# A transformer block on one core: score due times kept until issue, x loaded in eight parts

## The chip, the core and the metric

The kernel runs on one core of one Trainium2 chip. The time is the device time of one execution in microseconds (us); the median of three runs is compared. The engines are TensorE (PE), VectorE (DVE), ScalarE (ACT), GpSimd (POOL) and SyncE (SP, which issues the DMAs).

## The reference

One block of a transformer in bf16: attention with 32 heads on 2,048 tokens of width 640 (20 per head), then a gated MLP with hidden width 1,728. B_x is not read.

```python
x = A_x
h = x + _A_ref(_layernorm(x), A_wqkv, A_wo)
    # q, k, v = split(x @ wqkv); p = softmax(q k^T * 20**-0.5); o = p v; o @ wo
h2 = h + _B_ref(_layernorm(h), B_w_gate, B_w_up, B_w_down)
    # (gelu(x @ w_gate) * (x @ w_up)) @ w_down
```

## The kernel before

The program is written by a planner in the kernel file. Every operation is given to `op` with an engine, a planned duration, a priority (a low number goes first), what it reads and writes, and the PSUM banks that it takes and gives back. `Sched.schedule` plays the engines forward in planned time and lays down one order for each engine; `emit` then writes each engine's instructions in that order, with semaphore waits where an operand comes from another engine. So the order on each engine is fixed when the program is built. On the chip an engine that is late delays what stands behind it.

**Front.** x is loaded by `load_x` in four DMAs of four token tiles (128 tokens each), in the order XORD, followed by the weights. Tiles are normalized (statistics of tiles 0 to 10 on DVE, of 11 to 15 on ACT, by `act_stats`), transposed on PE and copied out by ACT or DVE (XN_DVE). K of the first head group is projected for all tokens, a bound for the exponent is worked out from it (`sel0`, `q_bound0`, key ("qo", 0, 0)), and then the first scores can be made. While x comes in, PE runs WN matmuls on zeros (line 607) wherever it has nothing else. HOLD, Q1_HOLD, V_HOLD and K1_AFTER say which of the next K, Q and V projections or copies wait for the bound or for an earlier copy.

**Attention.** Tokens (as queries) are cut into eight chunks (SIZES), and each chunk with a group of heads into slots, 32 in all; several tables (QK_LEAD, PE_AGE, SD_AGE, SD_ROW, D_SLOT, SUMS, D_RING, D_SPAN) have one entry for each slot. A score tile is 128 keys by 512 queries and fills one PSUM bank. Scores are made by PE in "row" mode (line 1059), units alternating between banks 0 to 2 and banks 3 and 4; one ACT instruction takes the exp of a whole unit, 1,536 or 1,024 columns, straight from PSUM, and gives its banks back. So score n+2 can be made when exp n has ended, and has to be there when exp n+1 ends. Of the tiles, 348 go to DVE, which builds the exponential from integer tricks (line 972 and four terms after it; SUMS says how many pairs of terms DVE adds up, which saves PE a PV pass). Such a tile has its scores in one of the banks 5 and 7 or, as D_RING says, in the third bank of a three-bank unit, whose exp is then a short one. PV (line 437 on PE, into bank 6) runs in "col" mode.

**The due time.** PE is also filled with background: projections for later chunks, output projection and MLP of the chunk before (`post`, lines 740, 1314, 1383). To keep it from being in the way of scores, the planner holds a time `due`, and skips a PE operation that would run across it:

```python
if e == "pe" and due is not None and o.prio[0] > 0 and t < due < t + o.dur + (MODE_SWITCH[e] ...):
    skipped.append((p, i))
...
if e == "act":
    act_end = max(act_end, t) + o.dur + ACT_GAP
    due = act_end + (0.917 if o.dur > 1.2 else 1.344) - at(QK_LEAD) if o.mode == "exp" else None
```

It is set anew each time that an operation is issued to ACT. When PE has nothing that it may start, it may run filler matmuls on zeros (`warm`, `pad`), which keep its recent activity above a share.

**After each chunk.** `post` makes the output projection, the layer norm (P_ADD and P_ST are the priorities of its DVE steps), the transposes (on PE for the chunks in XP_PE, by a DMA for the others) and the MLP. The last chunk's `post` runs behind the last exp.

Of the kernel before, what the change touches and what calls it, by code (L numbers as in the profile page):

```python
# [18 lines left out]
DRAIN = {"pe": 0.165, "act": 0.118, "dve": 0.085, "pool": 0.05, "sp": 0.0}  # L19
WARM_WIN, WARM_MIN = 3.4, 0.5  # L20
PAD_WIN, PAD_MIN = 3.4, 0.42
QK_LEAD = (0.68, 0.72, 0.65, 0.6, 0.65, 0.65,) + (0.72,) * 8 + (0.65,) * 3 + (0.72,) * 6 + (0.68,) * 9
ACT_GAP = .012
PE_AGE = (2.5, 3.0, 5.0, 5.0, 2.5,) + (1.0,) * 4 + (2.0,) + (5.0,) * 3 + (3.0,) * 8 + (1.5,) * 6 + (3.5, 3.0,) + (1.5,) * 3
SD_AGE = (0.6, 0.6, 0.3,) + (0.6,) * 6 + (0.8,) + (0.6,) * 3 + (0.5, 0.6, 1.0, 0.3, 0.6, 0.8, 0.6, 1.0, 0.5, 1.0, 1.0, 0.5,) + (0.6,) * 7
SD_ROW = (0,) * 5 + (1.0,) + (0.6,) * 3 + (1.5, 0.6, 0.6, 1.5,) + (0.6,) * 16 + (1.0, 0.6, 0,)
STOP = None


# [1 line left out]
MODE_SWITCH = {"pe": .098, "act": 1.28}  # L31
# [20 lines left out]
class Sched:  # L52
# [47 lines left out]
    def schedule(self):  # L100
# [11 lines left out]
        mode = {e: None for e in ENGINES}  # L112
# [13 lines left out]
        at = lambda v: v[cur] if isinstance(v, tuple) else v  # L126
        total = len(ops)
        scores = sum(o.eng == "pe" and o.mode == "row" for o in ops)
        while done < total:
            assert events, "no operation can start"  # L130
            t = heapq.heappop(events)
# [4 lines left out]
            for e in ENGINES:  # L136
# [8 lines left out]
                while ready[e]:  # L145
                    p, i = heapq.heappop(ready[e])
                    o = ops[i]
                    got = []
                    if e == "pe" and due is not None and o.prio[0] > 0 and t < due < t + o.dur + (MODE_SWITCH[e] if mode[e] not in (None, o.mode) else 0):
                        skipped.append((p, i))  # L150
                        if due not in events:
                            heapq.heappush(events, due)
                        if len(skipped) >= 60:
                            break
                        continue
                    for bk in o.acq:
                        for b in bk.allowed if scores else bk.allowed + bk.after:
                            if owner[b] is None and free_at[b] <= t + 1e-9 and b not in got and b not in kept:
                                got.append(b)
                                break  # L160
                        else:
                            got = None
                            break
                    if got and o.mode == "row" and 0 < p[0] < 1 and scores > 1 and t - o.ready < (
                            at(SD_AGE) if mode[e] != "row" else at(SD_ROW) if row_end[o.rows[0]] > max([row_start + 0.01] + [freed[b] for b in got]) + 0.02 else 0):
                        skipped.append((p, i))
                        continue
                    if got is None:

                        if p[0] == 0:  # L170
                            kept.update(bk.allowed[0] for bk in o.acq)
                        skipped.append((p, i))
                        continue
                    skipped.append((p, i))
                    if chosen is None:
                        chosen, banks = o, got
                        if e != "pe" or p[0] < 1 or p[0] == P_NOW or o.mode == mode[e] or t - o.ready > at(PE_AGE):
# [16 lines left out]
                if chosen is None:  # L194
                    if e == "pe" and self.warm is not None:
                        while recent and recent[0][0] < t - WARM_WIN:
                            recent.popleft()
                        fb = [b for b in self.warm_banks if owner[b] is None and free_at[b] <= t + 1e-9]
                        free7 = fb and all(hasattr(ops[d], "fin") and ops[d].fin + 0.06 <= t for d in self.warm_deps)
                        if sum(x for _, x in recent) < WARM_MIN * WARM_WIN and (free7 or live):  # L200
# [12 lines left out]
                            chosen = o  # L213
                            total += 1
                    if chosen is None:
                        continue
                o = chosen
                scores -= o.eng == "pe" and o.mode == "row"
                if o.tag and o.tag[0] == "S":
                    cur = self.slot_of[o.tag[1]]  # L220
                if e == "pe" and self.pad is not None and o.tag and o.tag[0] in ("O", "Oq"):
# [29 lines left out]
                if e == "act":  # L251
                    act_end = max(act_end, t) + o.dur + ACT_GAP
                    o.fin = act_end + o.lat
                    due = act_end + (0.917 if o.dur > 1.2 else 1.344) - at(QK_LEAD) if o.mode == "exp" else None
                heapq.heappush(events, free[e])
                for bk in o.rel:
                    b = bk.b
# [78 lines left out]
S = 2048  # L336
# [22 lines left out]
NTERM = len(TERMS)  # L359
PV_QUADS = 2  # L360
PR, PR2 = 13, 6
D_SLOT = (1,) + (3,) * 26 + (2, 3, 3, 0, 0,)
SUMS = (0,) + (1,) * 5 + (2, 0, 0, 1, 0,) + (1,) * 3 + (0, 1, 1, 2, 3, 1, 0, 1, 1, 0, 2, 2, 1, 0, 1, 0, 3, 0,)
HOP = 3.2
D_LAT = 0.3
RECIP_MAGIC = float(0x7EF311C3)
COL = 256
WN, WB, WW, WC = 76, (5, 4), 256, 32
VN = 4
D_RING = (9,) * 8 + (6,) * 20 + (12,) + (3,) * 3  # L370
D_FIRST = 0
D_SPAN = (16,) + (18,) * 13 + (17,) + (18,) * 4 + (19,) * 4 + (18,) * 7 + (17, 17,)
D0 = 8
P33 = ()
TANH_FROM = 768
GELU_A = 2.0 * 0.7978845608028654
# [6 lines left out]
P_V0 = 2.91  # L383
P_ON = 2.4
V_ACT = (0, 3)
XN_DVE = (8, 10, 13, 15)
VP = (0, 2, 5, 8)
V1 = ((0, 0, 0, 0, 0, 0, 0, 0, 1, 1, 1, 1, 1, 1, 1, 1), (2, 2, 2, 2, 3, 3, 3, 3, 3, 3, 3, 3, 4, 4, 4, 4))
# [27 lines left out]
def bass_sequential_preLN__mha_block__glu_gated_geglu__prompt_kernel(  # L416
# [12 lines left out]
    with ExitStack() as es:  # L429
# [13 lines left out]
        def c_act(n):  # L443
            return 0.052 + n * 0.000833
# [258 lines left out]


        def act_stats(t0, n):
            for t in sorted(range(t0, t0 + n), key=lambda t: (XORD.index(t // 4), t)):
                for f, k in ((ACT.Copy, 0), (ACT.Square, 1)):
                    op("act", I("activation", junk, x_sb[:, t, :], f, accum_out=asum[:, k, t - t0:t - t0 + 1]), 0.86, 1.4,
                       reads=[f"x{t // 4}"], writes=["junk", ("as", t)])
# [8 lines left out]
        for t0, n in GROUPS:  # L718
            if (t0, n) == AG:
                act_stats(t0, n)  # L720
            else:
                for t in range(t0, t0 + n):
                    ln_stats(x_sb[:, t, :], t, [f"x{t // 4}"], P_BG)
            ln_rsqrt(t0, n, P_RS, sqrt=True)
            for t in range(t0, t0 + n):
                e_ops.append(ln_apply("dve", x_sb[:, t, :], xn_p[:, t % 4, :], ("xnp", t % 4), t, [f"x{t // 4}"], P_PRO))
# [696 lines left out]
        for s_, (c, gs) in enumerate(slots):  # L1423
# [37 lines left out]
            if gs[-1] == NG - 1:  # L1461
# [39 lines left out]
```

## Time and profile before

| | us |
|---|---|
| median of 3 runs (lowest, highest) | 867.11 (866.93, 867.78) |
| profiled execution, its time | 867.46 |
| profiled execution, span of its instructions | 865.7 |
| PE busy | 835.9 |
| ACT busy | 839.4 |
| DVE busy | 748.5 |
| first exp starts | 33.00 |
| table load behind the last exp starts | 842.41 |

The granted TensorE clock reads 1.00 throughout. The groups name an instruction by its line, but line 437 is a helper that issues most instructions of ACT, DVE and SP, so the names of the tiles say more: `pts` and `rege` out of `ps` on ACT are exps, `rege` or `qt_all` out of `ps` on line 972 are tiles of DVE, `ps` out of `pts`, `rege` or `qt_all` with `v_all` on PE is PV, and `ps` out of `kt_all,zer` is filler.

### The profile page before, as it was taken

How to read it: one execution, taken by the hardware profiler on the slowest of the kernel's cores; microseconds unless marked ns; L12 is line 12 of the kernel's file. 1: busy time of each engine (PE TensorE's matmuls, PEld its weight loads, DVE VectorE, ACT ScalarE, POOL GpSimd, SP SyncE). 2: the span in 40 equal slices, each digit the busy share in tenths (PEclk: the TensorE clock that was granted, in tenths of full speed). 3: DMA queues.
4: the chain of work that ended last, by engine and by line, in shares of the span. 5: the costliest groups of instructions: out<-in, count | busy, mean ns of one | idle time of the engine just before them, and what ended most of it. 6: DMA issues, size and time to landing. Idle time of an engine off the chain costs nothing.

```text
span 865.7 us, 35516 instructions
## 1 busy us (share of the span) xinstructions
PE 835.9 (97%) x16187; PEld 420.8 (49%) x16219; DVE 748.5 (86%) x1371; ACT 839.4 (97%) x806; POOL 93.7 (11%) x268
## 2 busy tenths in 40 slices
PE   7999999999999899999999999999999999999998
PEld 5533332322344344445455555555554556666667
DVE  8859999999898899797899989999999897998344
ACT  7899999999999999999999999999999999999992
POOL 5001111110001210101002010011102110010000
DMA  7211122123102442001110201010101201020000
GB/s 274 84 50 57 32 71 61 46 71 93 53 4 67 128 146 80 16 18 36 53 42 16 36 8 61 5 35 17 49 19 24 58 8 31 19 48 11 2 18 17
DMA packets 47485, 42.54 MB, mean 49 GB/s; under 512 B 18628, under 2 KB 41952, under 8 KB 47336
## 3 DMA queue, kind: packets, MB, share of 16 engines
q1 hardware_dynamic: 47336, 40.27, 16.0%
q8 instruction: 127, 2.08, 1.0%
q14 instruction: 22, 0.18, 0.1%
HBM read 27.95 MB, written 10.26 MB: 44 GB/s over the span
## 4 chain that ended last, share of the span: by engine, by line
ACT 45%; PE 42%; DVE 11%; issue 1%; DVEq 0%
ACT pts L437 30%; ACT rege L437 14%; PE ps L1059 13%; PE ps L437 11%; PE ps L740 10%; PE ps L745 3%; DVE qt_all L437 2%; PE ps L887 2%; DVE rege L437 2%; DVE rege L972 2%; PE ps L1314 1%; DVE qt_all L972 1%; DVE stats L437 1%; ACT qt_all L437 1%; PE ps L1383 1%
## 5 line engine op out<-in xcount | busy, mean ns | idle before, releaser
L437 ACT ACTIVATE pts<-ps 128x1024 bf16<-128x1024 f32 (+1 forms) x496 | 558.3, 1232 | 2.9 <-PE ps L1059 2.1
L1059 PE MATMUL ps<-qt_all,kt_all 32*128 32x256 bf16 (+2 forms) x4096 | 307.1, 273 | 11.2 <-ACT pts L437 5.2
L437 ACT ACTIVATE rege<-ps 128x1024 bf16<-128x1024 f32 (+1 forms) x222 | 247.6, 1192 | 0.4 <-PE ps L1059 0.2
L1059 PEld LDWEIGHTS ps<-qt_all,kt_all 32*128 32x128 bf16 x4096 | 104.2, 92 | 198.1 <-ACT pts L437 83.0
L972 DVE TENSOR_SCALAR rege<-ps 128x512 int16<-128x512 f32 x220 | 148.2, 683 | 19.4 <-PE ps L1059 18.1
L437 PE MATMUL ps<-rege,v_all 128*21 128x256 bf16 (+2 forms) x2201 | 140.3, 286 | 1.3 <-DVE rege L437 0.5
L437 PE MATMUL ps<-pts,v_all 128*21 128x256 bf16 (+2 forms) x2403 | 124.7, 273 | 1.0 <-DVE osb L437 0.8
L740 PE MATMUL ps<-rege,regw 128*32 128x256 bf16 (+1 forms) x2600 | 120.5, 296 | 1.5 <-DVE rege L972 0.5
L972 DVE TENSOR_SCALAR qt_all<-ps 128x512 int16<-128x512 f32 x128 | 86.5, 682 | 11.9 <-PE ps L1059 11.4
L437 DVE TENSOR_SCALAR rege<-rege 128x2048 int16<-128x2048 int16 x141 | 94.5, 686 | 2.5 <-PE ps L437 1.9
L740 PEld LDWEIGHTS ps<-rege,regw 128*32 128x32 bf16 x2600 | 60.4, 96 | 34.6 <-issue 20.1
L437 PEld LDWEIGHTS ps<-rege,v_all 128*21 128x21 bf16 x2201 | 54.1, 91 | 42.7 <-issue 25.2
L437 PEld LDWEIGHTS ps<-pts,v_all 128*21 128x21 bf16 x2403 | 57.0, 91 | 26.1 <-issue 18.4
L740 PE MATMUL ps<-regw,rege 128*32 128x320 bf16 x1296 | 68.1, 301 | 0.7 <-issue 0.4
L437 DVE TENSOR_SCALAR qt_all<-qt_all 128x2048 int16<-128x2048 int16 (+4 forms) x113 | 65.4, 589 | 2.8 <-ACT qt_all L437 1.1
L437 PE MATMUL ps<-qt_all,v_all 128*21 128x256 bf16 (+1 forms) x1264 | 56.4, 264 | 0.8 <-DVE qt_all L437 0.8
L437 DVE TENSOR_SCALAR qt_all<-rege 128x2048 int16<-128x2048 int16 x80 | 53.8, 684 | 1.5 <-PE ps L437 0.9
L745 PE MATMUL ps<-regw 128*128 128x512 bf16 x176 | 52.5, 383 | 2.0 <-issue 1.1
L437 POOL TENSOR_SCALAR rn<-rc 128x16 int32<-128x16 int32 x22 | 6.7, 305 | 393.3 <-DMA rc<-sums 393.1
L1368 DVE TENSOR_TENSOR rege<-rege,ps 128x512 bf16<-128x512 bf16 (+2 forms) x53 | 35.0, 661 | 13.0 <-PE ps L740 6.6
L1314 PE MATMUL ps<-rege,regw 128*128 128x128 bf16 (+1 forms) x420 | 41.0, 238 | 0.0
L740 PEld LDWEIGHTS ps<-regw,rege 128*32 128x32 bf16 x1296 | 30.3, 96 | 19.3 <-issue 11.8
(139 smaller groups left out, 806.2 us busy)
## 6 DMA issues: line engine op xcount, KB each, us to landing
bsum<-rsums SPq DMA_DIRECT2D x88, 64.0 KB, 2.0
rege<-in_A_x_dram SPq DMA_DIRECT2D x5, 640.0 KB, 5.9
q_rows<-regw SPq DMA_DIRECT2D x20, 128.0 KB, 1.7
out_dram<-rege SPq DMA_DIRECT2D x15, 160.0 KB, 1.8
regw<-in_B_w_gate_dram SPq DMA_DIRECT2D x5, 432.0 KB, 3.3
regw<-in_B_w_up_dram SPq DMA_DIRECT2D x5, 432.0 KB, 3.4
kt_all<-k_rows SPq DMA_DIRECT2D x12, 160.0 KB
qt_all<-q_rows SPq DMA_DIRECT2D x12, 160.0 KB
```

Source lines behind the costliest of these rows:

```text
L437: return lambda eng: getattr(eng, method)(*args, **kwargs)
L740: return [lambda eng, j=j: eng.matmul(out()[32 * j:32 * j + 32], l[:, 32 * j:32 * j + 32], r, start=start, stop=stop, tile_position=(0, 32 ...
L745: fn = col4(lambda: bank(bk, n), l, r, k == 0, k == len(steps) - 1) if col else lambda eng, l=l, r=r, k=k: eng.matmul(bank(bk, n), l, r, s ...
L887: w_readers.append(op("pe", lambda eng, i=i, kt=kt, a=a: eng.matmul(bank(bk)[:, i * w:i * w + w], xnT[:, a, kt * 128:(kt + 1) * 128], wv[: ...
L972: d_ops.append(op("dve", lambda eng: eng.tensor_scalar(v[:, 512 * h:512 * h + 512], bank(b), EXP_MUL, -32000.0, ALU.mult, ALU.max), c_dve( ...
L1059: return lambda eng: eng.matmul(out()[:, kk * nq:(kk + 1) * nq], kt_all[32 * j:32 * j + 32, g, kt * 128:(kt + 1) * 128], qt_all[32 * j:32 ...
L1314: lambda eng, a=a, f=f, fi=fi: eng.matmul(bank(bk)[:, fi * nq:(fi + 1) * nq], w[:, a, F0[f]:F0[f] + 128], hnT[:, a, 128 * tb:128 * tb + nq ...
L1368: hdone.append(op("dve", lambda eng, bu=bu, fv=fv, w=w: eng.tensor_tensor(fv, fv, bank(bu, w), ALU.mult), c_dve(w), p, reads=[ku] + hkeys( ...
L1383: f == NF - 1) if cl else lambda eng, f=f, o=o, bk=bk, w0=w0, w1=w1: eng.matmul(
```

## The change

- **Due time.** A table `needed` holds the due time of each score by its number, and a score that is issued takes the next one out, so that it stands until that score is issued. The length of the running exp comes from the list of units (`sc.pace`). For GRACE = 0.05 us from the due time on, PE starts no other operation either. QK_LEAD goes from 0.60 to 0.72 down to 0.50 to 0.60. WARM_DUE, which would hold filler matmuls off the due time, is 0.
- **x** is loaded in eight DMAs of two tiles, in the order XORD = (0, 6, 1, 7, 2, 3, 5, 4).
- **WN**, the zero matmuls in front, goes from 76 to 60.
- **Tables.** One tile group for DVE moves from slot 18 to slot 23 (D_SLOT), SUMS rises by one in slots 0, 8 and 17 and falls by one in 19, D_RING rises from 6 to 9 in slots 8, 9, 12 and 13, D0 goes from 8 to 0, and a few entries of PE_AGE, SD_AGE, SD_ROW and D_SPAN change.
- **Order of the front and of `post`.** HOLD 1 to 3 (the second K's copies wait for the bound's end), Q1_HOLD 1 to 0, K1_AFTER 2 to 0, V_HOLD 6 to 4, XN_DVE and V1 changed, P_ADD 0.6 to 1.8, P_ST 1.9 to 0.7, and chunk 6 leaves XP_PE, so that its transpose is a DMA.

```diff
-QK_LEAD = (0.68, 0.72, 0.65, 0.6, 0.65, 0.65,) + (0.72,) * 8 + (0.65,) * 3 + (0.72,) * 6 + (0.68,) * 9
+QK_LEAD = (0.55,) * 9 + (0.5,) + (0.55,) * 9 + (0.5,) + (0.55,) * 10 + (0.6, 0.6,)
+GRACE = 0.05
+WARM_DUE = 0
...
-                    if e == "pe" and due is not None and o.prio[0] > 0 and t < due < t + o.dur + (MODE_SWITCH[e] if mode[e] not in (None, o.mode) else 0):
+                    if e == "pe" and due is not None and o.prio[0] > 0 and (
+                            t < due < t + o.dur + (MODE_SWITCH[e] if mode[e] not in (None, o.mode) else 0) or
+                            GRACE and due <= t < due + at(GRACE)):
...
+                n_exp += o.mode == "exp"
+                if o.tag and o.tag[0] == "S":
+                    n_qk += 1
+                    if GRACE:
+                        due = needed.pop(n_qk, None)
...
-                    due = act_end + (0.917 if o.dur > 1.2 else 1.344) - at(QK_LEAD) if o.mode == "exp" else None
+                    d = act_end + ((0.917 if o.dur > 1.2 else 1.344) if not GRACE or n_exp >= len(self.pace) else self.pace[n_exp]) - at(QK_LEAD) if o.mode == "exp" else None
+                    if GRACE and d is not None and n_qk <= n_exp:
+                        needed[n_exp + 1] = d
+                    elif not GRACE or d is not None:
+                        due = d
...
+        sc.pace = [c_act(512 * len(x)) + ACT_GAP + 0.005 for x in units]
...
-D_SLOT = (1,) + (3,) * 26 + (2, 3, 3, 0, 0,)
-SUMS = (0,) + (1,) * 5 + (2, 0, 0, 1, 0,) + (1,) * 3 + (0, 1, 1, 2, 3, 1, 0, 1, 1, 0, 2, 2, 1, 0, 1, 0, 3, 0,)
+D_SLOT = (1,) + (3,) * 17 + (2,) + (3,) * 4 + (4,) + (3,) * 3 + (2, 3, 3, 0, 0,)
+SUMS = (1,) * 6 + (2, 0, 1, 1, 0,) + (1,) * 3 + (0, 1, 1, 3, 3, 0, 0, 1, 1, 0, 2, 2, 1, 0, 1, 0, 3, 0,)
-WN, WB, WW, WC = 76, (5, 4), 256, 32
+WN, WB, WW, WC = 60, (5, 4), 256, 32
-D_RING = (9,) * 8 + (6,) * 20 + (12,) + (3,) * 3
+D_RING = (9,) * 10 + (6, 6, 9, 9,) + (6,) * 14 + (12,) + (3,) * 3
-D0 = 8
+D0 = 0
-XP_PE = (0, 6)
-HOLD = 1
+XP_PE = (0,)
+HOLD = 3
-K1_AFTER = 2
-Q1_HOLD = 1
-V_HOLD = 6
+K1_AFTER = 0
+Q1_HOLD = 0
+V_HOLD = 4
-XORD = (0, 3, 1, 2)
+XORD = (0, 6, 1, 7, 2, 3, 5, 4)
-P_ADD = 0.6
-P_ST = 1.9
+P_ADD = 1.8
+P_ST = 0.7
...
-            load(x_sb[:, 4 * i:4 * i + 4, :], x_hbm[512 * i:512 * (i + 1), :].rearrange("(t p) d -> p t d", p=128),
-                 f"x{i}", 5.1 + 1.8 * k)
+            load(x_sb[:, 2 * i:2 * i + 2, :], x_hbm[256 * i:256 * (i + 1), :].rearrange("(t p) d -> p t d", p=128),
+                 f"x{i}", 4.2 + 0.9 * k)
```

More of the change, by code (lines that the diff above doesn't have):

```diff
@@ L21 @@
 PAD_WIN, PAD_MIN = 3.4, 0.42
-QK_LEAD = (0.68, 0.72, 0.65, 0.6, 0.65, 0.65,) + (0.72,) * 8 + (0.65,) * 3 + (0.72,) * 6 + (0.68,) * 9
+QK_LEAD = (0.55,) * 9 + (0.5,) + (0.55,) * 9 + (0.5,) + (0.55,) * 10 + (0.6, 0.6,)
+GRACE = 0.05
+WARM_DUE = 0
 ACT_GAP = .012
-PE_AGE = (2.5, 3.0, 5.0, 5.0, 2.5,) + (1.0,) * 4 + (2.0,) + (5.0,) * 3 + (3.0,) * 8 + (1.5,) * 6 + (3.5, 3.0,) + (1.5,) * 3
-SD_AGE = (0.6, 0.6, 0.3,) + (0.6,) * 6 + (0.8,) + (0.6,) * 3 + (0.5, 0.6, 1.0, 0.3, 0.6, 0.8, 0.6, 1.0, 0.5, 1.0, 1.0, 0.5,) + (0.6,) * 7
-SD_ROW = (0,) * 5 + (1.0,) + (0.6,) * 3 + (1.5, 0.6, 0.6, 1.5,) + (0.6,) * 16 + (1.0, 0.6, 0,)
+PE_AGE = (2.5, 3.0, 5.0, 5.0, 2.5,) + (1.0,) * 4 + (2.0, 5.0, 5.0,) + (3.0,) * 9 + (1.5,) * 6 + (3.5, 3.0,) + (1.5,) * 3
+SD_AGE = (0.6, 0.6, 0.3,) + (0.6,) * 6 + (0.8,) + (0.6,) * 3 + (0.5, 0.6, 1.0, 0.3, 0.6, 0.8, 0.6, 1.0, 0.5, 1.0, 1.0, 0.5,) + (0.6,) * 5 + (0.3, 0.6,)
+SD_ROW = (0,) * 5 + (1.0,) + (0.6,) * 3 + (1.5, 0.6, 0.6, 1.5,) + (0.6,) * 11 + (1.0,) + (0.6,) * 4 + (1.0, 0.6, 0,)
 STOP = None
@@ L128, in schedule @@
         scores = sum(o.eng == "pe" and o.mode == "row" for o in ops)
+        n_qk = n_exp = 0
+        needed = {}
         while done < total:
@@ L148, in schedule @@
                     got = []
-                    if e == "pe" and due is not None and o.prio[0] > 0 and t < due < t + o.dur + (MODE_SWITCH[e] if mode[e] not in (None, o.mode) else 0):
+                    if e == "pe" and due is not None and o.prio[0] > 0 and (
+                            t < due < t + o.dur + (MODE_SWITCH[e] if mode[e] not in (None, o.mode) else 0) or
+                            GRACE and due <= t < due + at(GRACE)):
                         skipped.append((p, i))
-                        if due not in events:
+                        if t < due and due not in events:
                             heapq.heappush(events, due)
+                        if t >= due and due + at(GRACE) not in events:
+                            heapq.heappush(events, due + at(GRACE))
                         if len(skipped) >= 60:
@@ L199, in schedule @@
                         free7 = fb and all(hasattr(ops[d], "fin") and ops[d].fin + 0.06 <= t for d in self.warm_deps)
-                        if sum(x for _, x in recent) < WARM_MIN * WARM_WIN and (free7 or live):
+                        x = t + 0.215 + (MODE_SWITCH[e] if not (live and (mode[e] == "col" or not free7)) else 0)
+                        if WARM_DUE and due is not None and t < due < x:
+                            if due not in events:
+                                heapq.heappush(events, due)
+                        elif sum(x for _, x in recent) < WARM_MIN * WARM_WIN and (free7 or live):
                             o = Op()
@@ L367 @@
 COL = 256
-WN, WB, WW, WC = 76, (5, 4), 256, 32
+WN, WB, WW, WC = 60, (5, 4), 256, 32
 VN = 4
-D_RING = (9,) * 8 + (6,) * 20 + (12,) + (3,) * 3
+D_RING = (9,) * 10 + (6, 6, 9, 9,) + (6,) * 14 + (12,) + (3,) * 3
 D_FIRST = 0
-D_SPAN = (16,) + (18,) * 13 + (17,) + (18,) * 4 + (19,) * 4 + (18,) * 7 + (17, 17,)
-D0 = 8
+D_SPAN = (16,) + (18,) * 12 + (17,) * 4 + (18, 18,) + (19,) * 4 + (18,) * 7 + (17, 17,)
+D0 = 0
 P33 = ()
@@ L385 @@
 V_ACT = (0, 3)
-XN_DVE = (8, 10, 13, 15)
+XN_DVE = (9, 11, 13, 15)
 VP = (0, 2, 5, 8)
-V1 = ((0, 0, 0, 0, 0, 0, 0, 0, 1, 1, 1, 1, 1, 1, 1, 1), (2, 2, 2, 2, 3, 3, 3, 3, 3, 3, 3, 3, 4, 4, 4, 4))
+V1 = ((0, 0, 0, 0, 0, 0, 0, 0, 0, 0, 0, 0, 0, 0, 0, 0), (2, 2, 2, 2, 2, 2, 2, 2, 3, 3, 3, 3, 3, 3, 3, 3))
 X_LAT = 3.0
@@ L705, in act_stats @@
         def act_stats(t0, n):
-            for t in sorted(range(t0, t0 + n), key=lambda t: (XORD.index(t // 4), t)):
+            for t in sorted(range(t0, t0 + n), key=lambda t: (XORD.index(t // 2), t)):
                 for f, k in ((ACT.Copy, 0), (ACT.Square, 1)):
                     op("act", I("activation", junk, x_sb[:, t, :], f, accum_out=asum[:, k, t - t0:t - t0 + 1]), 0.86, 1.4,
-                       reads=[f"x{t // 4}"], writes=["junk", ("as", t)])
+                       reads=[f"x{t // 2}"], writes=["junk", ("as", t)])
             m = mv[:, t0:t0 + n, 0]
@@ L722, in bass_sequential_preLN__mha_block__glu_gated_geglu__prompt_kernel @@
                 for t in range(t0, t0 + n):
-                    ln_stats(x_sb[:, t, :], t, [f"x{t // 4}"], P_BG)
+                    ln_stats(x_sb[:, t, :], t, [f"x{t // 2}"], P_BG)
             ln_rsqrt(t0, n, P_RS, sqrt=True)
             for t in range(t0, t0 + n):
-                e_ops.append(ln_apply("dve", x_sb[:, t, :], xn_p[:, t % 4, :], ("xnp", t % 4), t, [f"x{t // 4}"], P_PRO))
+                e_ops.append(ln_apply("dve", x_sb[:, t, :], xn_p[:, t % 4, :], ("xnp", t % 4), t, [f"x{t // 2}"], P_PRO))
                 if t in XD:
```

## The prediction

> **What bounds the kernel now.** I read the page first, then the waits of ScalarE (ACT), the groups by shape, the chain, the timeline around single stalls, and the stages at both ends.
>
> ```profile
> span 865.7 us, 35516 instructions
> PE 835.9 (97%) x16187; PEld 420.8 (49%) x16219; DVE 748.5 (86%) x1371; ACT 839.4 (97%) x806; POOL 93.7 (11%) x268
> ...
> ACT pts L437 <- PE ps L1059: 2.1, 6, 0.6
> ...
> 33.00 3.71 ACT L437 ACTIVATE pts<-ps 128x1536 bf16<-128x1536 f32 x3 [0.64 <-PE ps L1059]
> 842.41 1.28 ACT L437 ACT_TABLE_LOAD   x1
> ```
>
> ACT and TensorE (PE) both read 97%, so the page alone doesn't say which one sets the end. The two last rows cut the run in three: 33.0 us ahead of the first exp, 809.4 us of attention (33.00 to 842.41), and a tail of 865.7 - 842.4 = 23.3 us. The waits of ACT name only 2.1 us of waiting for scores (line 1059). But ACT overlaps the end of one instruction with the start of the next, so a short delay shows as a longer pitch and not as idle time. The pitch stands in the chain, the number of exps in the groups by shape:
>
> ```profile
> 270.80 5.97 ACT pts L437 x5
> 276.77 2.75 ACT rege L437 x3
> 279.52 5.44 ACT pts L437 x5
> ...
> 287.21 5.01 ACT pts L437 x5
> ...
> L437 ACT ACTIVATE pts<-ps 128x1024 bf16<-128x1024 f32 x300 | 306.9, 1065 | 1.2 <-PE ps L1059 0.9
> L437 ACT ACTIVATE pts<-ps 128x1536 bf16<-128x1536 f32 x196 | 291.4, 1487 | 1.8 <-PE ps L1059 1.2
> L437 ACT ACTIVATE rege<-ps 128x1024 bf16<-128x1024 f32 x154 | 156.2, 1061 | 0.1
> L437 ACT ACTIVATE rege<-ps 128x1536 bf16<-128x1536 f32 x68 | 101.1, 1487 | 0.3 <-PE ps L1059 0.2
> L437 ACT ACTIVATE qt_all<-qt_all 128x1024 f16<-128x1024 f16 x13 | 14.2, 1101 | 0.0
> L437 ACT ACTIVATE rege<-rege 128x2048 bf16<-128x2048 bf16 x4 | 7.4, 1903 | 0.0
> L437 ACT ACT_TABLE_LOAD x8 | 10.3, 1283 | 0.9 <-PEq L1486 0.8
> ```
>
> Runs of five differ by their mix: 5.01 is four short exps (1,024 columns) and one long (1,536), 5.44 is three and two. The difference makes long minus short 0.43 us, so the short pitch is 0.916 us (three give the row's 2.75) and the long 1.346. Three long and two short would be 5.87; the row with 5.97 holds 0.10 of waiting that no idle column shows. All exps at these pitches take 454 x 0.916 + 264 x 1.346 = 771.2 us. Other ACT work between the two marks is 14.2 + 7.4 + half of the table loads (5.1) and a few small groups that I put at 5 us together; less an overlap of 0.15 us (1.065 - 0.916) for some 21 of them, about 29 us. 809.4 - 771.2 - 29 leaves about 9 us of score stalls in pieces of 0.05 to 0.6 us. That pool is what the new due time can reach. One such piece:
>
> ```profile
> 86.96 1.99 ACT L437 ACTIVATE rege<-ps 128x1024 bf16<-128x1024 f32 x2
> 88.96 1.45 ACT L437 ACTIVATE pts<-ps 128x1536 bf16<-128x1536 f32 x1
> ...
> 87.76 0.61 PE L437 MATMUL ps<-rege,v_all 128*21 128x512 bf16 x8
> 88.20 0.39 PE L437 MATMUL ps<-pts,v_all 128*21 128x512 bf16 x4
> 88.52 0.60 PE L1059 MATMUL ps<-qt_all,kt_all 32*128 32x512 bf16 x4
> ```
>
> Two short exps start at 86.96 and should end 2 x 0.916 later, at 88.79; the next exp starts at 88.96, 0.17 late. The banks for it came free near 87.88, when the first of the two ended. PE then finished eight PV matmuls, ran four more at 88.20, and only then the scores at 88.52, 0.64 after the release. From scores to exp is 0.44 (88.52 to 88.96), so with a short exp running the scores must start within 0.916 - 0.44 = 0.47 us of the release.
>
> **The change, part by part.** *The due time.* Before, each exp that the planner issues overwrites it, so it is lost just when the banks come free; a tanh wipes it. And it guesses the running exp's length from the last one's: after a short exp it says 1.344 less QK_LEAD (0.60 to 0.72), about 0.65 after the release, which is where this row sits (0.64). The 95 units of which VectorE (DVE) takes one bank are short exps where the guess says long, so some 190 guesses of 718 are wrong. After, the length comes from the unit list, the due time stays until that score is issued, and it is 0.905 + 0.017 - 0.55 = 0.37 us after the release for a short exp. The four matmuls at 88.20 (0.32 after it, until 0.64) would be refused; the scores would start at 88.20, and the 0.17 us go. But 0.37 against 0.47 leaves only 0.10 us for PE to run behind plan, less than where the old rule aimed after a long exp (0.917 less 0.65 to 0.72, 0.2 to 0.27 after the release). So I take 5 of the 9 us: bounds 0 (all is lateness of PE against the plan) and 9.
>
> What waits instead is PE's background, and DVE behind it. It is covered while PE has slack:
>
> ```profile
> 500.00:600.00 100.00, 98.37 (x2474) 1.00 0.10 27
> 600.00:700.00 100.00, 99.05 (x2355) 1.00 0.13 33
> ...
> sum 809.00, PE 787.11; mean PE 87.46
> ...
> 500.00:600.00 100.00, 0.60 (x8) 1.00 0.10 27
> 600.00:700.00 100.00, 0.40 (x4) 1.00 0.13 33
> ...
> sum 809.00, PE 22.73; mean PE 2.53
> ```
>
> The upper rows are PE's stages, the lower ones those of the filler matmuls on zeros. Idle 809.0 - 787.1 = 21.9 and filler 22.7 make 44.6 us, 0.062 us per score of 719; but from 500 to 700 only 1.63 + 0.95 + 1.00 = 3.6 us. What is put off there moves to later stages.
>
> *Tables.* Counted from the tables, 2,048 tiles still split into 1,700 for ACT and 348 for DVE; ACT gets 719 exps for 718 (455 of two banks, 263 of three, one of a single bank): a bank costs 0.43, so the fixed part of an exp is 0.916 - 2 x 0.43 = 0.06 us, and one exp more adds that. Pair sums rise from 27 to 29:
>
> ```profile
> L437 DVE TENSOR_TENSOR qt_all<-qt_all 128x2048 bf16<-128x2048 bf16 x9 | 10.9, 1213 | 0.0
> ```
>
> DVE gains 2 x 1.21 = 2.4 us, PE loses two groups of four PV matmuls (0.22 each, half of 87.76 to 88.20). At 86% busy DVE hides it; uncovered it would cost 2.4. WARM_DUE is 0, so that branch does nothing. The other age and span tables only reorder: 0, bounds -1 and +1.
>
> *The front.*
>
> ```profile
> 0.78 3.03 SPq L437 DMA_DIRECT2D rege<-in_A_x_dram  x4
> 6.55 0.48 DVE L437 MEMSET v_all<- 128x512 bf16 x1 [1.84 <-issue]
> 6.65 1.22 DVE L437 BATCH_NORM_STATS2 stats<-rege 128x6 f32<-128x320 bf16 x3
> 7.23 0.74 ACT L437 ACTIVATE rege<-rege 128x640 bf16<-128x640 bf16 x1 [1.36 <-DMA rege<-in_A_x_dram]
> ...
> 2.92 7.97 PE L607 MATMUL ps<-zer,ident 128*128 128x256 bf16 x47 [2.92 <-POOL ident L437]
> 12.95 0.45 PE L662 MATMUL ps<-ident,rege 128*128 128x128 bf16 x5 [2.06 <-DVE rege L437]
> 14.91 3.05 PE L607 MATMUL ps<-zer,ident 128*128 128x256 bf16 x26
> ...
> 9.00:10.00 1.00, 1.00 (x12) 0.88 (x10) 1.00 (x4) 0.78 (x2) 0.81 (x4) 1.00 1.06 408
> ```
>
> The four parts of x move at 408 GB/s (9 to 10 us), so a part of 320 KB takes 0.8 us where one of 640 took 1.6. ACT waits 1.36 us for its first tile, now in the second half-size part: that goes. DVE carries the chain up to about 20 us; it stood 1.84 us ahead of a memset that waits for no data, so an earlier x may or may not bring it forward. Bounds 0 and -1.84; I take -0.9. SP issues four more DMAs, 0.76 us each by the first row (3.03 for 4), and the weights queue 3 us further back; the same bytes lie ahead of them, so they land as before. The new holds (K and V copies after the first bound) move DVE work behind the first exp: within the same bounds. Of the 16 dropped zero matmuls I expect the last to go, those of the run of 26 at 14.91, where PE waits anyway: 0.
>
> A rule speaks against the eight parts. The Trainium skill ("DMA: Bandwidth & Descriptors", section Bandwidth) says to batch DMAs to 1 MiB for 75% of peak, and its table lies at 138 GB/s for 64 KB and 341 for 1 MB. By an estimate from it, 220 GB/s at 320 KB, the 2.6 MB of x would land 5 us later, and the gain of the front would be 0. The trace disagrees for queued parts: 408 GB/s at 640 KB.
>
> *The tail.*
>
> ```profile
> 803.05 0.45 DVE L437 TENSOR_SCALAR xn_t<-rege,mu,rs 128x640 bf16<-128x640 bf16 x1
> ...
> 814.88 0.49 DVE L1388 TENSOR_TENSOR rege<-ps,rege 128x320 bf16<-128x320 f32 x1 [0.38 <-PE ps L1383]
> rege<-xn_t SPq DMA_TRANSPOSE x10, 3.0
> ...
> 851.52 7.98 PE L1314 MATMUL ps<-rege,regw 128*128 128x128 bf16 x140
> ```
>
> Chunk 6 is transposed by a DMA (3.0 us to land, so near 806.5) in place of PE and a DVE copy, no quicker than 1 us after 803.5. PE is still at chunk 5's down projection at 814.88, which hides the 2 us between; uncovered they are +2. The last chunk's MLP (851.52 on) is unchanged. Tail 0, bounds -0.6 and +2 for background left over.
>
> Sum: -5.0 - 0.9 + 0.06 + 0 = -5.8. The profiled execution took 867.46 us for its span of 865.7, so 861.6; the median of the runs lies 0.35 lower: **861.3**.
>
> **Rivals.** *Given back (0.17).* The stalls go, but the 3.6 us of slack between 500 and 700 are used up and the background is worked off after the last exp. For it: PE at 99% there. Against: 44.6 us free in all. A fifth of the run's stalls would be made up there and at most the 3.6 us missing slack comes back, I say 3: 864.5. *Slower (0.15).* PE held free costs more than it saves. A loss of r per score uses 719 r out of 44.6 us of slack, or 39.6 once the stalls are gone; it decides from 0.055 us. At 0.068 it leaves 9.3 us of background behind the last exp, where PE is already full, less 5.8: 870.6. Against: the due time (0.37) lies behind the release, so a 0.22 us operation mostly fits. *No effect (0.14).* The stalls come from PE running late against its plan, not from the plan. For it: the matmuls at 88.20 start 0.32 after the release, when no plan with the scores ready would pick them. Only the front gains: 866.3. *Cold PE (0.05).* The 47 zero matmuls from 2.92 run at 5.9 per us on the whole and at 12 between 9 and 10 (granted clock 1.00), so PE was at half rate for about 5 us. If fewer of them let it fall back, half of that, 2.5 us, is lost ahead of the first exp: 863.8. The Trainium skill ("TensorE: Matmul & The Clock Gate", part 1) states such a rule: half clock after an idle window of about 3.4 us. By the trace, PE was not slow after its 2.06 us gap (26 zero matmuls in 3.05 us at 14.91), which is why the chance is small.
>
> **How the numbers follow.** The forecast has 0.49, its own range 857 to 865 (9 or 1 us of stalls, front 0 to -1.8). 0.2% is 1.7 us, about what a measurement of this kernel can tell from no change. Faster: 0.49, of "given back" 0.13, of "no effect" 0.04, cold 0.05: 0.71. Same: 0.12 from those two. Slower: 0.15 and 0.02: 0.17. The range 857.0 to 867.5 leaves out the slower case and a little below.
>
> **What would show it.** Right: fewer and smaller steps like 5.97 against 5.87 in ACT's chain, attention of about 804.5 us, first exp near 32.1, tail within 1 us of 23.3. PE rows with PV at 0.3 us behind a release and scores at 0.64 should be gone. Wrong: attention unchanged (PE's lateness), a tail of 26 us or more (given back), filler or idle PE up by over 30 us (reserved stretch too dear), zero matmuls well under 8 per us after 13 us (cold).

## Result and the profile after

The changed kernel took **870.49 us** (median of seven runs, 870.27 to 870.70) against 867.11 (866.66 to 867.78): 1.0034 of the time before, 95% interval 1.0025 to 1.0044. It is slower by 3.4 us; 861.3 was forecast. The profiled execution has the median's time.

The page of the changed kernel, its span and its engines:

```profile
span 868.8 us, 35317 instructions
PE 829.0 (95%) x16080; PEld 417.3 (48%) x16115; DVE 749.4 (86%) x1372; ACT 837.9 (96%) x807; POOL 90.9 (10%) x268
```

ACT in its timeline, at the first exp and at the table load behind the last one, the marks that the prediction used:

```profile
30.68 1.28 ACT L458 ACT_TABLE_LOAD   x1
37.13 4.20 ACT L458 ACTIVATE pts<-ps 128x1024 bf16<-128x1024 f32 x4 [5.17 <-PE ps L1080]
...
844.77 1.28 ACT L458 ACT_TABLE_LOAD   x1
```

ACT's waits (in total, times, longest):

```profile
ACT pts L458 <- PE ps L1080: 6.2, 4, 5.2
```

| us | before | after | difference | forecast |
|---|---|---|---|---|
| ahead of the first exp | 33.00 | 37.13 | +4.13 | -0.9 |
| attention, first exp to table load | 809.41 | 807.64 | -1.77 | -4.9 |
| tail | 23.33 | 23.99 | +0.66 | 0 |
| span | 865.74 | 868.76 | +3.02 | -5.8 |

So attention did get shorter, and the loss is one wait of 5.17 us at the first exp.

For the small waits I took the starts and ends of all exps from both traces. Where nothing holds an exp up, it starts 0.904 us behind the start of a short one (1,024 columns) and 1.330 behind that of a long one (1,536). The ends follow at another pitch: 0.917 us for a short exp and 1.344 for a long one, within 0.005 us of it in 406 of the 441 short and 206 of the 258 long exps after that directly follow another exp. So the starts run ahead of the ends, and a late start need not delay an end. Of the changed kernel, ACT's timeline:

```profile
193.10 2.45 ACT L458 ACTIVATE rege<-ps 128x1024 bf16<-128x1024 f32 x2
195.33 5.22 ACT L458 ACTIVATE pts<-ps 128x1024 bf16<-128x1024 f32 x5
200.42 2.40 ACT L458 ACTIVATE rege<-ps 128x1536 bf16<-128x1536 f32 x2
```

The middle row is four short exps and a long one. At the pitch of starts the next one would follow 4.95 us later; it starts 5.09 later, so it is 0.14 late. But the first row ends at 195.55 and the middle one at 200.55, 5.00 apart, where 4 x 0.917 + 1.344 = 5.01 are due: no end was delayed. Of 128 starts that were over 0.03 us late before, 55 delayed no end by more than that. What costs time is therefore counted at the ends: what the distance of two ends has over its pitch, if more than 0.03 us, I call a delay. One that follows a short exp is put down by the exp before that one:

| delays of ends: number, us | before | after |
|---|---|---|
| after two short exps | 34, 4.37 | 16, 1.84 |
| after a long and a short one | 38, 4.12 | 45, 5.04 |
| all | 73, 8.55 | 61, 6.88 |

Attention less its delays is 800.9 us before and 800.8 after: the delays make the difference. (The expectations below count late starts: 53 of 6.7 us in all after two short exps before, 43 of 4.2 after.)

**The first exp.** TensorE in its timeline:

```profile
30.48 0.38 PE L892 MATMUL ps<-regw,sel 128*128 128x512 bf16 x1
30.72 1.25 PE L766 MATMUL ps<-regw 128*128 128x512 bf16 x5
31.81 0.79 PE L908 MATMUL ps<-regw 128*128 128x160 bf16 x9
32.51 3.41 PE L766 MATMUL ps<-regw 128*128 128x512 bf16 x15
35.85 0.39 PE L872 MATMUL ps<-regw,sel 128*32 128x512 bf16 x1
36.17 0.59 PE L908 MATMUL ps<-regw 128*128 128x160 bf16 x6
36.69 0.61 PE L1080 MATMUL ps<-qt_all,kt_all 32*128 32x512 bf16 x5
```

VectorE, the step that writes the bound into Q:

```profile
30.97 0.75 DVE L896 SCALAR_TENSOR_TENSOR qt_all<-ps,off,qt_all 128x512 bf16<-128x512 f32 x1 [0.36 <-PE ps L892]
```

SyncE's queue, the DMAs that put K into the layout of the scores:

```profile
25.93 12.20 SPq L458 DMA_DIRECT2D kt_all<-regw  x16
```

The same two places before the change, in the timelines of TensorE and of SyncE's queue:

```profile
32.57 0.60 PE L1059 MATMUL ps<-qt_all,kt_all 32*128 32x512 bf16 x5
...
24.72 11.98 SPq L437 DMA_DIRECT2D kt_all<-regw  x16
```

The bound stands at 31.72, and the scores could have followed. But from 31.81 on PE makes 31 other matmuls, nearly all of projections, and begins the scores at 36.69, 4.1 us later than before. The reason is in the DMAs of K. In the first slot DVE's one block of keys is block 8, the ninth of 16, and D0 says with which unit DVE's first tile goes. With D0 = 8 the first unit has three ACT tiles, all of early keys. With D0 = 0 it has two and DVE's tile of block 8 as its third bank. That block's keys lie in the third of four parts of K, whose copies are numbers 9 to 12 of the 16: at 0.76 us each they are issued from 32.0 to 35.1. The order on PE is written by a planner that knows this, so it puts the first score matmuls, five together, at 36.69 and the projections ahead of them.

### The profile page after: what moved, and what is told of

Its sections match the earlier page's. It is cut to its first block, busy times and chain, and to the rows that moved or that the text cites. A ratio compares the mean times of both kernels' runs of the same rounds, so it can differ in the third digit from the quotient of the medians.

```text
span 868.8 us, 35317 instructions
## 1 busy us (share of the span) xinstructions
PE 829.0 (95%) x16080; PEld 417.3 (48%) x16115; DVE 749.4 (86%) x1372; ACT 837.9 (96%) x807; POOL 90.9 (10%) x268
## 4 chain that ended last, share of the span: by engine, by line
ACT 64%; PE 31%; DVE 4%; issue 1%; DVEq 0%
ACT pts L458 44%; ACT rege L458 19%; PE ps L1080 9%; PE ps L761 8%; PE ps L458 7%; PE ps L1335 2%; PE ps L908 2%; PE ps L766 2%; ACT qt_all L458 2%; DVE stats L458 1%; PE ps L1404 1%; DVE rege L458 1%; DVE qt_all L458 1%; DVE rege L993 0%; PE ps L683 0%
## 5 line engine op out<-in xcount | busy, mean ns | idle before, releaser
L458 PE MATMUL ps<-rege,v_all 128*21 128x256 bf16 (+2 forms) x2159 | 136.5, 287 | 0.6 <-DVE rege L458 0.3
L458 PE MATMUL ps<-pts,v_all 128*21 128x256 bf16 (+2 forms) x2417 | 122.3, 273 | 0.1
L458 PEld LDWEIGHTS ps<-rege,v_all 128*21 128x21 bf16 x2159 | 51.2, 91 | 42.2 <-issue 26.2
L458 PEld LDWEIGHTS ps<-pts,v_all 128*21 128x21 bf16 x2417 | 55.0, 91 | 25.7 <-issue 17.9
L1389 DVE TENSOR_TENSOR rege<-rege,ps 128x512 bf16<-128x512 bf16 (+2 forms) x53 | 34.9, 660 | 13.6 <-PE ps L761 6.8
L1335 PE MATMUL ps<-rege,regw 128*128 128x128 bf16 (+1 forms) x420 | 38.6, 238 | 0.1
```

Source lines behind the costliest of these rows:

```text
L458: return lambda eng: getattr(eng, method)(*args, **kwargs)
L1335: lambda eng, a=a, f=f, fi=fi: eng.matmul(bank(bk)[:, fi * nq:(fi + 1) * nq], w[:, a, F0[f]:F0[f] + 128], hnT[:, a, 128 * tb:128 * tb + nq ...
L1389: hdone.append(op("dve", lambda eng, bu=bu, fv=fv, w=w: eng.tensor_tensor(fv, fv, bank(bu, w), ALU.mult), c_dve(w), p, reads=[ku] + hkeys( ...
```

## The experiments

The first four runs put D0 on trial, from both sides, and with it the due rule.

**d0_8**: after, with `D0 = 0` -> `D0 = 8`.

> The changed kernel with D0 put back from 0 to 8, so that the first units hold no tile of VectorE. Theory (K part): with D0 = 0 the first unit's third bank holds a tile whose keys are block 8, in the third of the four K parts, whose copies SyncE issues ninth to twelfth; the first scores wait for it. Then the first exp comes back from 37.1 to 31.5 to 33.0 us. Rival (order of the front): the late start comes from x in eight parts and the new holds; then the first exp stays above 35. For the total: if only the front moves, 870.5 - 4 to - 5, 865.5 to 866.5; if the planner's whole order moves with it and the tables no longer fit it, attention or tail grow by several us and the total says nothing about the front.

**before_d0_0**: before, with `D0 = 8` -> `D0 = 0`.

> The kernel before with D0 = 0 alone. Theory (K part): the first exp moves from 33.0 to 36 to 37.5 us although x still comes in four parts and all holds are the old ones. Rival (order of the front): it stays within 0.5 us of 33.0. Total, if only the front moves: 867.1 + 3 to + 4.5.

**kb0**: after (D0 = 0), DVE's block in slot 0 being key block 0, which lies in the first part of K.

```diff
             d_kb[s_] = [mine[(2 * i + 1) * len(mine) // (2 * n)] for i in range(n)]
+            if s_ == 0:
+                d_kb[s_] = mine[0:1]
```

> The changed kernel, D0 still 0, but VectorE's block of the first slot is key block 0, in the first K part, in place of block 8. The first unit still gives its third bank to VectorE. Theory (K part): the first exp comes at 31.5 to 33.0 us, as with D0 = 8. Rival (a tile of VectorE in the first unit is itself what costs, through its bank or VectorE's load): it stays at 36 to 37.

**d0_8_old_due**: after, with D0 = 8, `GRACE = 0` (the old due rule) and QK_LEAD of before.

> The changed kernel with D0 = 8 and the old due-time rule (GRACE = 0 and the old QK_LEAD). Beside the run with D0 = 8 it shows the rule at the same front. Theory of the prediction: the new rule takes 2 to 5 us of score stalls from the attention, so here attention is 2 to 5 us longer, with more steps behind short exps that follow short ones (before 53 of them, 6.7 us; after 43, 4.2 us). Rival (PE sets the end, stalls are what is left over): attention and tail together are within 1.5 us of the run with the new rule.

The first exp in ACT's timeline of d0_8, before_d0_0 and kb0:

```profile
32.36 5.97 ACT L458 ACTIVATE pts<-ps 128x1536 bf16<-128x1536 f32 x5 [0.38 <-PE ps L1080]
```

```profile
37.24 6.03 ACT L437 ACTIVATE pts<-ps 128x1024 bf16<-128x1024 f32 x6 [4.28 <-PE ps L1059]
```

```profile
32.37 6.03 ACT L458 ACTIVATE pts<-ps 128x1024 bf16<-128x1024 f32 x6 [0.38 <-PE ps L1082]
```

| | median us (range) | ratio to before | first exp | attention | tail |
|---|---|---|---|---|---|
| d0_8 | 886.43 (886.11-889.83) | 1.0218 [1.0196, 1.0240] | 32.36 | 816.2 | 35.8 |
| before_d0_0 | 882.42 (881.62-884.77) | 1.0167 [1.0149, 1.0186] | 37.24 | 807.5 | 35.2 |
| kb0 | 890.71 (888.14-891.21) | 1.0252 [1.0234, 1.0271] | 32.37 | 821.5 | 35.7 |
| d0_8_old_due | 884.93 (883.91-885.23) | 1.0189 [1.0172, 1.0206] | 32.36 | 816.1 | 34.9 |

The first exp is settled: D0 = 0 makes it 4.77 us later in the one kernel (32.36 to 37.13) and 4.24 in the other (33.00 to 37.24). kb0 shows the mechanism: D0 stays at 0, DVE still has the third bank of the first unit, only the block of keys that it gets in slot 0 is another, and the exp comes at 32.37. Apart from D0 the front gained 0.64 us (33.00 to 32.36).

The totals went the other way: all four are 14 to 22 us above before (868.3 us in the runs beside them), though two of them only undo a fault. The loss is elsewhere, in a tail of 35 us and, but for before_d0_0, in single long waits. Of d0_8, ACT's timeline:

```profile
109.97 2.37 ACT L458 ACTIVATE pts<-ps 128x1024 bf16<-128x1024 f32 x2 [2.35 <-PE ps L1080]
...
871.36 0.60 ACT L1358 ACTIVATE qt_all<-ps 128x512 bf16<-128x512 f32 x1 [9.77 <-PE ps L1335]
```

9.77 us of waiting in the tail: PE works off the MLP of the chunk before there, until it comes to the last one's. One changed number moves the whole order behind it, and the other tables (ages, spans, sums) no longer fit. The expectation of d0_8 named this case, with several us and not 16 for it.

d0_8_old_due was to show the rule at the same front. Attention is 816.1 us against 816.2 with the new rule, and with the tail it is 1.1 us shorter: its rival came true, and the 2 to 5 us of the theory did not.

The next four runs crossed the due rule with the tables and took two parts alone.

**old_due**: after with `GRACE = 0` and QK_LEAD of before (D0 = 0 and all other tables of after).

> The changed kernel (D0 still 0, all its tables) with the old due-time rule: GRACE = 0 and the old QK_LEAD. Theory of the prediction (the rule saves score stalls by itself): attention 2 to 5 us longer than the 807.6 us of the changed kernel, tail within 1 us of its 24.0. Rival (rule and tables belong together: any other order of the background leaves PE's work unfinished): attention about 816 and a tail of 33 to 36 us, as in the four runs ahead of this one, which is no measure of the rule.

**due_only**: before with the new due rule and its QK_LEAD, nothing else.

> The kernel before with the new due-time rule and its QK_LEAD, all other tables and the front as before. Theory of the prediction: attention 2 to 5 us shorter than 809.4, first exp 33.0, tail 23.3, in all 862 to 865 us. Rival (rule and tables belong together): the score stalls do not fall, attention 812 to 820 and the tail 30 us or more, in all above 875.

**grace_0**: after with `GRACE = 0.05` -> `0.0001`: the due time is kept, the free stretch behind it is gone.

> The changed kernel with the stretch left free cut from 0.05 us to 0.0001, the kept due times as they are. The order of PE differs in some 150 of 2,444 rows. If the free stretch does what it says, more score stalls and attention 0.5 to 1.5 us longer; if it does nothing, within 0.3 us of the changed kernel, 870.5.

**xp_6**: after with `XP_PE = (0,)` -> `(0, 6)`, as before: chunk 6 transposed on PE again.

> The changed kernel with chunk 6 transposed on PE again. Prediction: the DMA transpose is hidden, so within 0.3 us of 870.5, tail 24.0. Rival (the 3 us of the DMA transpose push chunk 6's MLP into the tail): tail 0.7 us shorter, 869.8.

| | median us (range) | ratio to before | first exp | attention | tail | delays after two short exps: number, us |
|---|---|---|---|---|---|---|
| old_due | 891.47 (890.26-893.80) | 1.0272 [1.0256, 1.0289] | 37.19 | 817.4 | 34.5 | 36, 7.3 |
| due_only | 883.08 (882.10-883.80) | 1.0172 [1.0158, 1.0186] | 33.54 | 815.5 | 31.4 | 26, 4.8 |
| grace_0 | 870.85 (870.59-871.05) | 1.0032 [1.0020, 1.0044] | 37.16 | 807.7 | 24.0 | 14, 2.0 |
| xp_6 | 870.75 (869.85-871.31) | 1.0029 [1.0018, 1.0041] | 37.19 | 808.4 | 23.9 | 16, 2.0 |

Rule and tables only go together: old with old 867, new with new 870, new rule on old tables 883, old rule on new tables 891. So "the rule alone" can't be read from a total, and the rivals of old_due and due_only came true. Its mark can be read, in the delays after two short exps that are under 0.3 us. Three pairs of runs differ in the rule alone:

| under 0.3 us: number, us | old rule | new rule |
|---|---|---|
| tables of before (before, due_only) | 32, 3.43 | 22, 1.76 |
| tables of after (old_due, after) | 31, 3.20 | 15, 1.52 |
| tables of after, D0 = 8 (d0_8_old_due, d0_8) | 32, 3.54 | 23, 2.40 |

So the rule takes 1.1 to 1.7 us of these small delays whatever the tables are. With the longer ones the sums are 4.37 and 4.78, 7.26 and 1.84, 6.05 and 7.37 us: the longer ones come with tables that don't fit, under either rule, and hide what the rule does. The free stretch is worth nothing (grace_0 within 0.4 us of after), and so is XP_PE.

Of due_only, ACT's longest wait shows how a mismatch costs; no delay of before is above 0.62 us:

```profile
138.38 2.37 ACT L458 ACTIVATE pts<-ps 128x1024 bf16<-128x1024 f32 x2 [5.63 <-PE ps L1080]
```

Two more runs asked where the delays come from that the rule left, and what the eight parts of x give. The planner counts 0.905 + 0.012 us for a short exp and 1.332 + 0.012 for a long one, 0.012 being ACT_GAP. That is the pitch of the ends, 0.917 and 1.344. The expectation of gap takes the pitch of the starts for the one to plan by. That was a wrong reading: with 0.002 the planner's clock runs ahead of the ends, by 719 x 0.010 = 7.2 us in all.

**gap**: after with `ACT_GAP = .012` -> `0.002`.

> Kernel after with ACT_GAP = 0.002 in place of 0.012: the planner adds less to the end of each exp, so its clock for ACT runs 719 x 0.010 = 7.2 us less behind the measured pitch (0.905 us a short exp, 1.331 a long one, where none waits). Theory A (most of the 119 stalls of after, 13.0 us, are of about 0.1 us because the plan puts scores on a slow clock and ACT catches up with it): 70 stalls or fewer, and 6 to 8 us in those under 0.3 us. Theory B (they come from TensorE running late against its plan): about 120 stalls as in after, and some of them longer, since nothing is left for the lateness. The tables are not set anew for the changed order, so by the runs so far the tail behind the last exp is expected at 31 to 36 us instead of 24 under both, and the total at 872 to 885; the stalls decide, not the total. First exp at 36 to 37.5.

**x8_only**: before with x in eight parts in the order of after (load_x and the steps that name its parts), nothing else.

> Kernel before with x loaded in eight parts in the order of after, and nothing else (DVE's first tile stays key block 8). Theory (the eight parts give the 0.64 us by which the first exp comes earlier than in before once D0 is back at 8): first exp at 32.2 to 32.6 against 33.00. Rival (that gain is of the held-back K and V copies and of V1 and XN_DVE, not of the parts): first exp at 32.9 to 33.1, and above it if the four further DMA issues on SP delay the weights. The order behind it is another than the tables were set for: tail 29 to 36, total 875 to 885 under both.

One run each: gap 880.69 us (first exp 37.61, attention 808.9, tail 32.5), x8_only 881.58 (32.84, 816.6, 30.4), before beside them 868.04. *gap:* late starts under 0.3 us fell from 114 with 10.7 us to 71 with 6.1, as theory A had it, but with the longer ones there were 81, and the limit of 70 was missed; some got longer, as theory B had it. At the ends, delays under 0.3 us fell from 57 with 5.0 us to 13 with 1.4, but eight longer ones with 7.3 us took the place of four with 1.8. In all they rose from 6.9 to 8.7 us, and attention from 807.6 to 808.9. Of gap, two of the longer ones:

```profile
438.50 3.28 ACT L458 ACTIVATE pts<-ps 128x1536 bf16<-128x1536 f32 x3 [2.29 <-PE ps L458]
...
637.28 4.20 ACT L458 ACTIVATE pts<-ps 128x1536 bf16<-128x1536 f32 x4 [1.78 <-PE ps L458]
```

*x8_only:* 32.84 against 33.00, so the eight parts give 0.16 us; this lies nearer the rival. The other 0.48 of the 0.64 is then left for the held K and V copies and the moved steps of the front, which were not tried alone.

The last two runs have tables set anew, by a search over written-out orders, for either rule with the small gap.

**before_tuned**: before (old rule, four parts) with `ACT_GAP = 0.002`; QK_LEAD, ages, SD_ROW, spans, SUMS, D_RING, `P_ADD = 0.7`, `P_ST = 1.2` and `D0 = 12` set anew.

> Kernel before (old due rule, x in four parts) with ACT_GAP = 0.002 and its tables set anew for that clock by a search over the order written out (QK_LEAD, PE_AGE, SD_AGE, SD_ROW, SUMS, D_RING, D_SPAN, the priorities P_ADD and P_ST, one tile of D_SLOT; D0 = 12, which still lies in the second of the four K parts as key block 8 does). Theory A (the slow clock makes the small stalls, and the long tails and waits of the runs so far come from tables that do not fit the order): before has 121 stalls under 0.3 us, 12.1 us; at the rate of the run with ACT_GAP alone (10.7 to 6.1 us) 7 us are left, so attention about 804 instead of 809.4, first exp 33 to 34, tail 23 to 25, total 861 to 864. Theory B (any order but the two given ones costs 12 us or more, or the smaller gap brings as many longer waits): 875 or more, with single waits of ACT above 1 us and a tail above 30.

**after_tuned**: after (new rule, eight parts) with the same kind of tables set anew, `ACT_GAP = 0.002`, `GRACE = 0.02`, `D0 = 8`, `V_HOLD = 6`, `P_ADD = 0.6`.

> Kernel after (new due rule with a free stretch of 0.02 us, x in eight parts) with D0 = 8, V_HOLD = 6, ACT_GAP = 0.002 and its tables set anew for them in the same way. Theory A (the three causes found are all there is: D0 at the first exp, the slow clock at the small stalls, tables that do not fit at the tail and the long waits): first exp 32.4, attention 802 to 805, tail 23 to 25, total 859 to 863, at or below that of the retuned kernel before by up to 2 us, since the new rule cuts the stalls after two short exps by 2 us where the old one does not. Theory B (the new rule has a cost of its own, by holding TensorE free, that D0 only hid): attention above 807 or a tail above 27, and a total above that of the retuned kernel before by 2 us or more.

(The text on before_tuned calls D0 a place among the keys; it is the number of the unit, in slot 0, with which DVE's first tile goes. D_SLOT is as in before, though the text has a tile of it moved.)

| | median us (range) | ratio to before | first exp | attention | tail | delays: number, us |
|---|---|---|---|---|---|---|
| before_tuned | 867.59 (866.87-868.74) | 0.9991 [0.9982, 1.0000] | 34.23 | 808.0 | 23.3 | 52, 7.1 |
| after_tuned | 866.12 (865.17-866.81) | 0.9976 [0.9967, 0.9986] | 32.32 | 809.1 | 23.1 | 36, 8.3 |

Of after_tuned, the first exp, a long wait and the mark of the tail in ACT's timeline:

```profile
32.32 5.97 ACT L458 ACTIVATE pts<-ps 128x1536 bf16<-128x1536 f32 x5 [0.31 <-PE ps L1080]
...
569.67 1.94 ACT L458 ACTIVATE rege<-ps 128x1024 bf16<-128x1024 f32 x2 [2.00 <-PE ps L1080]
...
841.38 1.28 ACT L458 ACT_TABLE_LOAD   x1
```

The long tails are gone in both, so they were a matter of tables and not of any order but the given ones (theory B of before_tuned falls). after_tuned beats both kernels; it is 0.24% below before, which took 868.4 us beside it. In the profiled runs it gains at the front and in the tail, 0.68 and 0.22 us of its 1.25 us of span, and 0.35 in attention. Both expectations of 859 to 864 were missed, and always at the same place: attention stayed at 808 to 809 (and the first exp of before_tuned, 34.23, lies above its 33 to 34). Of after_tuned's theory B one mark came (attention above 807) and the others did not. Its total is 1.5 us below before_tuned's, as theory A had it, but not for the reason given: its attention is 1.0 us longer, the delays after two short exps sum to 6.8 us against 4.1, and what makes it faster is a first exp 1.9 us earlier.

In before, after, gap and the two tuned kernels attention less its delays is 800 to 801 us, so 7 to 9 us are all that is to be had there: the delays are 8.6, 6.9, 8.7, 7.1 and 8.3 us, in this order. What stays open is where they come from. In gap a planner's clock that runs ahead of ACT turned many small delays into few large ones. That would fit TensorE running behind its plan, but it isn't shown; an experiment that makes TensorE's own work shorter was not run.

## Why the prediction was wrong, step by step

**The step that failed: "the other age and span tables only reorder: 0, bounds -1 and +1".** The prediction doesn't name D0; this term, with no other left for the rest of the tables, put it at nothing. D0 doesn't reorder; it changes what the first unit is made of, so that the first exp needs keys that the DMAs bring 4 to 5 us later. The runs put +4.2 to +4.8 us on it, more than the whole loss of 3.4. Everything for it stood in the kernel and the profile of before: DVE's block 8, the row of the 16 K copies in SP's queue (24.72, 11.98 us) and the first exp with three ACT banks at 33.00. I read that queue as something that the x DMAs are put ahead of, and did not ask which of its copies the first unit waits for.

**Stalls, -5.0 of a pool of 9.** The pool was right: its pitches, 0.916 and 1.346, are those of the ends, and the delays of before sum to 8.55 us. The reading of the row with 5.97 was not: that row runs from the start of its first exp to the end of its last one, and the others of that chain from end to end. Its five exps end at 276.77, and by ACT's timeline the next one starts at 276.62, 5.82 behind the first, which is the bare pitch of starts. There is no waiting in it. The gain was mis-sized, and this is the second step that failed: 1.7 us in delays, 1.77 in attention. The mechanism was right where it was shown, after two short exps, the case of the timeline at 86.96: 4.37 us became 1.84. After a long and a short exp, where the other half of the pool lies, nothing was gained (4.12 to 5.04). The prediction treated all stalls as one kind and as the plan's doing. Whether the rival "no effect", that PE runs late against its plan, holds for that half is not shown.

**Front, -0.9.** -0.64 without D0, within the bounds. ACT's wait for x went, and its first tile starts at 5.78 instead of 7.23, which fits the reading that not ACT but DVE carries the chain. In VectorE's timeline the row that stood at 6.55 has hardly moved:

```profile
6.54 0.48 DVE L458 MEMSET v_all<- 128x512 bf16 x1 [1.84 <-issue]
```

so of the 1.84 us nothing came through. SyncE's issue of the eight parts cost less than the 0.76 us each that I took from the four:

```profile
0.78 4.48 SPq L458 DMA_DIRECT2D rege<-in_A_x_dram  x8
```

That is 0.56 each, so the weights went out 1.45 us later, not 3. Nor did the first parts move at the rate of the larger ones, as the prediction took it. The row from 5 to 6 us, of before and of x8_only (the last number is what the core's DMAs moved, in GB/s):

```profile
5.00:6.00 1.00, 1.00 (x7) 0.72 (x5) 0.00 (x0) 0.88 (x1) 0.94 (x2) 1.00 1.07 393
...
5.00:6.00 1.00, 1.00 (x7) 0.73 (x5) 0.00 (x0) 1.00 (x2) 0.94 (x2) 1.00 1.02 288
```

By the rule of the Trainium skill quoted there ("DMA: Bandwidth & Descriptors", Bandwidth) the smaller parts should have brought x late. The trace agrees in the direction and not in the size: 288 GB/s in place of 393, and by the landings in the trace the last part of x is there at 11.27 us in x8_only and at 10.59 before, 0.7 us later and not 5. The first exp still came 0.16 us earlier.

**Tail, 0.** +0.66, within the bounds, but not for the reason weighed there: xp_6 has 23.94. In VectorE's timeline behind the last exp, after and (last row) before:

```profile
844.76 0.69 DVE L1389 TENSOR_TENSOR rege<-rege,ps 128x512 bf16<-128x512 bf16 x1 [1.29 <-PE ps L1335]
...
846.23 0.75 DVE L458 COPY osb<-ps 128x256 f32<-128x256 f32 x2
...
843.30 0.75 DVE L437 COPY osb<-ps 128x256 f32<-128x256 f32 x2
```

DVE waits 1.29 us for an up projection of the chunk before, and the last output sums are copied out 1.46 us behind the table load, where it was 0.89 (843.30 less 842.41). That is 0.57 of the 0.66: a little of "given back".

**The rivals.** "Slower" forecast 870.6, and 870.49 was measured, but by another mechanism: the nearness is luck. ("Given back" is 861.3 + 3 = 864.3, not 864.5.) Free and filler time of PE between 33 and 842 us, all PE work by stages and then the filler alone:

```profile
500.00:600.00 100.00, 95.25 (x2348) 1.00 0.11 29
600.00:700.00 100.00, 95.10 (x2123) 1.00 0.09 26
...
sum 809.00, PE 779.42; mean PE 97.43
```

```profile
33.00:842.00 809.00, 15.66 (x172) 1.00 0.16 44
```

Idle 29.6 and filler 15.7 make 45.3 us, where before had 44.6. PE is left free more between 500 and 700 (9.7 us, 2.6 before) and makes less filler, and grace_0 shows that the free stretch costs nothing. "Cold PE" didn't come: the zero matmuls behind 13 us run at 8.2 per us (TensorE's timeline):

```profile
14.89 1.83 PE L628 MATMUL ps<-zer,ident 128*128 128x256 bf16 x15
```

## What to carry to other kernels

Ask of each changed number whether it changes the order of the work or what the work consists of; the first use of data that arrives in parts has to be read against the queue that brings the parts. Where an order is written by a planner with tuned tables, a single edit on it measures the mismatch (10 to 21 us here) and not the edit: count the mark of the edit in the trace (small delays of one kind, the first exp), or set the tables anew for either side before comparing totals. And read the pace of an engine from the ends of its instructions. Counted at the starts, before had 14.6 us of stalls, counted at the ends 8.55, and only the second is time that could be had; the experiment gap was built on the first.

## What the runs showed of the hardware

ScalarE starts exps straight from PSUM 0.904 us (1,024 columns) or 1.330 us (1,536) apart, but they end 0.917 and 1.344 us apart. So their rows grow from one to the next (a short one reads 1.02 us at 221.50 of after and 1.14 at 232.24), and a start that is late by up to 0.19 us (at 134.00 of after) left the ends on their pitch. SyncE issues a DMA of 320 KB of x in 0.56 us and one of 640 KB in 0.76. Between 5 and 6 us, while x comes in, the core's DMAs moved 288 GB/s with x in parts of 320 KB (x8_only) and 393 with parts of 640 KB (before).
